# Moving VectorE's chord additions to GpSimd as 64-bit adds, and LN2's rstd to VectorE, in a fused attention and gated-MLP kernel

## The chip, the cores and the metric

The kernel runs on one core of one Trainium2 chip. The metric is device microseconds of one execution; lower is better. Each version is run several times and the median is quoted. A ratio is the mean time of one kernel's fast runs over that of the other's fast runs in the same rounds on the same chip, so it is not quite the ratio of the medians quoted beside it.

Names: PE is the matmul engine, ACT is ScalarE, DVE is VectorE, POOL is GpSimd. PSUM is the on-chip memory in which PE leaves its results here; SBUF is the one that holds the other tiles.

## The reference, cut to what matters

```python
h  = x + attention(layernorm(x), wqkv, wo)           # S = 2048, D = 512, 32 heads of 16
h2 = h + (sigmoid(g) * u) @ w_down                   # g, u = layernorm(h) @ w_gate, w_up;  F = 1792
```

Softmax runs over 32 heads of 2048 x 2048 scores. The exponentials of these scores are most of ACT's work. The first layernorm is called LN1 here, and the one on h is LN2. The rstd of a layernorm is one over the standard deviation of a row.

## The kernel before: the parts that matter

The scores of 128 keys by 512 queries make one *tile*. A *round* computes two or three tiles on PE. ACT exponentiates them in one instruction, or hands one tile of three to DVE. DVE builds its exponential from an integer trick. A first pass turns the score into the bits of an fp16 number. Two *chords*, the same bits plus a constant, are then added, and all three are multiplied by V with suitable weights, so their sum approximates the exponential. A DVE tile costs PE three multiplications where an ACT tile costs one.

```python
CHORDS, WEIGHT = (326, -332), 1.5625
...
def dexp_first(src, u, n):                  # first pass: PSUM scores -> int16
    ...
    nc.vector.tensor_scalar(out=J[:, 0, k, :], in0=src, scalar1=ZOFF, scalar2=0.0, op0=ALU.add, op1=ALU.max)
    T["D"] = max(T["D"], sc_end[n] + LAT) + 601
    ...
    uns = [Unit(u, J[:, s, k, :].bitcast(FP16), n, None if s else T["D"] + TAIL["D"],
                v=Vaug2 if s == 2 else Vaug) for s in range(3)]
    ...                                     # after up to four tiles: dexp_rest
def dexp_rest():
    ...
    def chord(s):                           # DVE adds the chord to k tiles at once
        nc.vector.tensor_scalar(out=J[:, s, 0:k, :], in0=J[:, 0, 0:k, :], scalar1=float(CHORDS[s - 1]),
                                scalar2=0.0, op0=ALU.add, op1=ALU.max)
        for i in range(k):
            quad[i][s].end = T["D"] + TAIL["D"]
    for s in (1, 2):
        chain.append((70 + 133 * k, lambda s=s: chord(s)))
```

The order of every engine's instructions is fixed when the program is built. A greedy scheduler in Python keeps a clock `T` per engine, adds an assumed cost for every instruction, and places next on PE whatever it believes to be ready. `Unit.end` is the time at which it believes an operand to be ready. On the chip, PE executes that order and waits wherever the belief was wrong. The assumed constants (601 ns, `70 + 133 * k`, `TAIL`) therefore decide the order.

```python
TAIL = {"A": 150.0, "D": 85.0, "G": 100.0}
def av_ready(loose):                        # which tiles may be multiplied by V now
    return [un for un in avq if un.u[:2] == gseq[st["cur"]] and un.end is not None
            and un.end + LAT <= T["P"] + loose]
```

The rstd of both layernorms is computed on GpSimd (an add, then a power of -0.5). GpSimd also makes the identity matrix at the start, on which everything depends.

## Time and profile before

781.5 us, median of 3.

| | busy us | share |
|---|---|---|
| PE | 730.5 | 94% |
| ACT | 735.3 | 94% |
| DVE | 708.5 | 91% |
| POOL | 29.8 | 4% |

The head of the profile's page: span, busy time of each engine, and the shares of the engines in the chain of waits that ended last.

```profile
span 779.7 us, 25718 instructions
...
PE 730.5 (94%) x11270; PEld 348.8 (45%) x11350; DVE 708.5 (91%) x1402; ACT 735.3 (94%) x780; POOL 29.8 (4%) x67
...
PE 48%; DVE 25%; ACT 21%; issue 5%; POOL 1%; DMA 0%; ACTq 0%; DVEq 0%
```

Three engines are nearly full, and the chain passes among them. PEld, the weight loads, has 11350 records and PE only 11270. 80 matmuls are missing from this trace, and their time reads as idle. The costliest groups on ACT and DVE (line, engine, operation, output and input, count, busy us, mean ns, idle before and its releasers):

```profile
L1346 ACT ACTIVATE pt<-PS 128x1024 f16<-128x1024 f32 (+1 forms) x516 | 544.5, 1161 | 10.9 <-PE PS L1031 4.3
L1202 DVE TENSOR_SCALAR J<-PS 128x512 int16<-128x512 f32 x545 | 360.2, 678 | 26.7 <-PE PS L1179 10.7
...
L1220 DVE TENSOR_SCALAR J<-J 128x2048 int16<-128x2048 int16 (+3 forms) x326 | 183.6, 594 | 0.8
```

L1220 is the work that the change moves: 326 chord additions, 183.6 us.

Busy time in stretches of 100 us (columns: stretch, its length, PE, PEld, DVE, ACT, POOL with instruction counts, PE clock, DMA share, GB/s):

```profile
300.00:400.00 100.00, 95.59 (x1640) 48.14 (x1646) 96.27 (x190) 98.24 (x105) 1.92 (x5) 1.00 0.21 62
600.00:700.00 100.00, 96.18 (x1676) 46.98 (x1680) 94.31 (x185) 97.79 (x103) 2.34 (x4) 0.98 0.18 54
```

The timelines of POOL and of ACT (start, duration, instruction):

```profile
0.73 0.20 POOL masks.py:197 MEMSET ident_bf<- 128x128 bf16 x1 [0.29 <-POOLq L1531]
1.01 0.29 POOL masks.py:199 TENSOR_SCALAR_AFFINE_SELECT ident_bf<-ident_bf 128x128 bf16<-128x128 bf16 x1
...
12.48 1.02 ACT L1346 ACTIVATE pt<-PS 128x1024 f16<-128x1024 f32 x1
```

The identity is ready at 1.3 us, and the first exponential starts at 12.48 us.

### The profile page before, as it was taken

The numbers are of one execution on the slowest core, as the hardware profiler recorded it, in microseconds if no ns is written. First come the engines' busy times: TensorE is split into PE (matmuls) and PEld (weight loads), VectorE is DVE, ScalarE is ACT, GpSimd is POOL, SyncE is SP. The second block draws the span as 40 slices with busy tenths as digits, with TensorE's granted clock in tenths as the row PEclk, the third lists the DMA queues.
The fourth block names the chain that finished last, engine by engine and source line by source line (L and its number), as shares of the span: only waits on it lengthen the run. The fifth ranks groups of instructions, "written<-read, shape, count | busy, mean of one in ns | idle before, by whom it ended". The sixth has DMA issues, their size and how long they took to land.

```text
span 779.7 us, 25718 instructions
## 1 busy us (share of the span) xinstructions
PE 730.5 (94%) x11270; PEld 348.8 (45%) x11350; DVE 708.5 (91%) x1402; ACT 735.3 (94%) x780; POOL 29.8 (4%) x67
## 2 busy tenths in 40 slices
PE   8899998988899999999999999999999999999997
PEld 3322223444454445544545455445543454345554
DVE  7987999999899899989999899998999999899863
ACT  5979999999999999999999999999999999999962
POOL 4300000000000000000000000100000000000000
PEclk9999999999999999999999999999999999999999
DMA  7000004000122103200211122101311123012160
GB/s 230 1 0 2 1 21 145 2 3 2 43 69 80 32 3 97 84 29 29 59 53 56 35 77 84 46 18 40 93 56 35 36 84 110 8 37 83 29 204 17
DMA packets 66806, 41.56 MB, mean 53 GB/s; under 512 B 3456, under 2 KB 66688, under 8 KB 66688
## 3 DMA queue, kind: packets, MB, share of 16 engines
q1 hardware_dynamic: 66400, 39.59, 17.1%
q8 instruction: 90, 1.47, 0.8%
q10 hardware_dynamic: 288, 0.26, 0.1%
q14 instruction: 28, 0.23, 0.1%
HBM read 37.75 MB, written 2.10 MB: 51 GB/s over the span
## 4 chain that ended last, share of the span: by engine, by line
PE 48%; DVE 25%; ACT 21%; issue 5%; POOL 1%; DMA 0%; ACTq 0%; DVEq 0%
ACT pt L1346 16%; PE PS L1031 16%; PE PS L1179 14%; DVE J L1202 11%; PE PS L770 8%; PE PS L788 5%; DVE J L1220 4%; PE PS L287 2%; DVE st L260 2%; DVE xs L1097 1%; ACT QTb L1346 1%; ACT xnT_83 L1346 1%; DVE hT L842 1%; ACT th L800 1%; DVE Vaug L296 1%
## 5 line engine op out<-in xcount | busy, mean ns | idle before, releaser
L1346 ACT ACTIVATE pt<-PS 128x1024 f16<-128x1024 f32 (+1 forms) x516 | 544.5, 1161 | 10.9 <-PE PS L1031 4.3
L1202 DVE TENSOR_SCALAR J<-PS 128x512 int16<-128x512 f32 x545 | 360.2, 678 | 26.7 <-PE PS L1179 10.7
L1179 PE MATMUL PS<-pt,Vaug 128*17 128x256 f16 (+1 forms) x2164 | 199.4, 279 | 3.6 <-DVE xs L1097 2.7
L1179 PE MATMUL PS<-J,Vaug 128*17 128x256 f16 (+1 forms) x2084 | 195.3, 279 | 4.3 <-DVE xs L1097 1.7
L1220 DVE TENSOR_SCALAR J<-J 128x2048 int16<-128x2048 int16 (+3 forms) x326 | 183.6, 594 | 0.8
L1179 PEld LDWEIGHTS <-Vaug 128*17 128x17 bf16 x4882 | 125.9, 90 | 74.0 <-issue 67.9
L1179 PE MATMUL PS<-J,Vaug_100 128*17 128x256 f16 (+1 forms) x1042 | 117.7, 279 | 0.7 <-DVE J L1220 0.6
L770 PE MATMUL PS<-xnT_82,wgu 128*128 128x256 bf16 x784 | 113.5, 275 | 0.6 <-DVE qd L699 0.2
L770 PEld LDWEIGHTS <-wgu 128*128 128x128 bf16 x784 | 63.9, 97 | 39.9 <-issue 34.3
L1179 PEld LDWEIGHTS <-Vaug_100 128*17 128x17 bf16 x1042 | 48.7, 90 | 27.4 <-issue 26.3
L1346 ACT ACTIVATE xnT_83<-PS 128x1024 f16<-128x1024 f32 (+1 forms) x51 | 57.0, 1119 | 0.2 <-PE PS L1031 0.2
L788 PE MATMUL PS<-wd,hT 128*128 128x512 bf16 x167 | 50.7, 383 | 3.4 <-issue 3.2
L1031 PEld LDWEIGHTS <-KT_86 32*128 32x128 bf16 x768 | 21.6, 91 | 61.4 <-issue 59.6
L1031 PEld LDWEIGHTS <-KT_87 32*128 32x128 bf16 x1024 | 25.5, 92 | 52.6 <-issue 50.7
L1031 PEld LDWEIGHTS <-KT_88 32*128 32x128 bf16 x1024 | 24.4, 92 | 50.3 <-issue 49.3
L1346 ACT ACTIVATE QTb<-PS 128x1024 f16<-128x1024 f32 x42 | 45.6, 1085 | 1.3 <-PE PS L1031 0.9
L800 ACT ACTIVATE th<-PS 128x512 f32<-128x512 f32 (+1 forms) x63 | 38.0, 603 | 7.5 <-DVE hT L783 6.7
L1031 PE MATMUL PS<-QT_92,KT_87 32*128 32x256 bf16 x512 | 38.6, 274 | 5.4 <-ACT pt L1346 3.5
L1031 PEld LDWEIGHTS <-KT_89 32*128 32x128 bf16 x1024 | 24.3, 92 | 42.0 <-issue 41.2
L1031 PE MATMUL PS<-QT_93,KT_87 32*128 32x256 bf16 x512 | 37.4, 272 | 2.8 <-ACT pt L1346 1.8
L1346 ACT ACTIVATE xnT_84<-PS 128x1024 f16<-128x1024 f32 (+1 forms) x36 | 38.8, 1091 | 0.9 <-PE PS L1031 0.8
L1031 PE MATMUL PS<-QT_95,KT_88 32*128 32x256 bf16 x512 | 37.2, 272 | 2.2 <-ACT pt L1346 1.7
(289 smaller groups left out, 808.4 us busy)
## 6 DMA issues: line engine op xcount, KB each, us to landing
wgu<-in_B_w_gate_dram SPq DMA_DIRECT2D x49, 256.0 KB, 3.0
wgu<-in_B_w_up_dram SPq DMA_DIRECT2D x49, 256.0 KB, 3.4
out_dram<-ob SPq DMA_DIRECT2D x16, 128.0 KB, 1.7
wd<-in_B_w_down_dram SPq DMA_DIRECT2D x1, 1792.0 KB, 9.3
xr<-in_A_x_dram SPq DMA_DIRECT2D x14, 128.0 KB, 3.6
J<-in_B_w_gate_dram SPq DMA_DIRECT2D x2, 768.0 KB, 4.5
J<-in_B_w_up_dram SPq DMA_DIRECT2D x2, 768.0 KB, 6.2
xb_111<-in_A_x_dram SPq DMA_DIRECT2D x2, 256.0 KB, 5.3
```

What stands on the lines that cost most here:

```text
L260: nc.vector.bn_stats(out=st[:], in_=src)
L287: nc.tensor.matmul(ps, lhsT=w_sb[:, d, p * P:(p + 1) * P], rhs=xnT[c][:, d, :], start=(d == 0), stop=(d == DC - 1))
L296: nc.vector.tensor_copy(out=Vaug[:, t, :, 0:DH], in_=ps.rearrange("p (h d) -> p h d", d=DH))
L770: nc.tensor.matmul(ps[:, 0:PARTS[r][2]], lhsT=w[:, d, :], rhs=hn_of(r)[:, d, :], start=(d == 0), stop=(d == DC - 1))
L788: nc.tensor.matmul(ps, lhsT=hT[:, f, i * P:(i + 1) * P], rhs=wd[:, f, :], start=(f == 0), stop=(f == FC - 1))
L800: nc.scalar.activation(out=th[:, 0:ps.shape[-1]], in_=ps, func=ACT.Tanh, scale=0.5)
L842: nc.vector.scalar_tensor_tensor(out=hT[:, f:f + k, 0:w], in0=th[f][:].rearrange("p (k n) -> p k n", k=k), scalar=1.0, in1=ps2.rearrange(" ...
L1031: nc.tensor.matmul(pss[:, ui, i * CW[qc]:(i + 1) * CW[qc]], lhsT=KT[g // 2][32 * j:32 * j + 32, k * P:(k + 1) * P], rhs=q[32 * j:32 * j + ...
L1179: nc.tensor.matmul(dst[32 * j:32 * j + VW, 0:w], lhsT=un.v[:, kt * SPAN[qc] + i, h, :], rhs=un.ap[:, i * w:(i + 1) * w], start=clears and ...
L1202: nc.vector.tensor_scalar(out=J[:, 0, k, :], in0=src, scalar1=ZOFF, scalar2=0.0, op0=ALU.add, op1=ALU.max)
L1220: nc.vector.tensor_scalar(out=J[:, s, 0:k, :], in0=J[:, 0, 0:k, :], scalar1=float(CHORDS[s - 1]), scalar2=0.0, op0=ALU.add, op1=ALU.max)
L1346: ex = nc.scalar.activation(out=pt, in_=pss[:, 0:wa, :], func=ACT.Exp, scale=AS)
```

## The change

The intent is to take the chords off DVE, which is 91% busy, and give them to GpSimd, which is 96% idle. The constant is added to four int16 values at once, as one 64-bit add. The first pass gets a floor of 332, so that no 16-bit field borrows from its neighbour. LN2's rstd leaves GpSimd and becomes six one-column DVE operations (a bit-trick guess and two Newton steps). After LN1, GpSimd does nothing but 64-bit adds.

```diff
+    def rstd_steps(dst, var):
+        ...                                  # guess(): v = var + eps; y = bits(v) * -0.5 + magic
+        def newton(i, s):
+            ...
+            nc.vector.tensor_scalar(out=t[:], in0=src, scalar1=src, scalar2=v[:], op0=ALU.mult, op1=ALU.mult)
+            nc.vector.tensor_scalar(out=out, in0=t[:], scalar1=3 * s * s, scalar2=src,
+                                    op0=ALU.subtract, op1=ALU.mult)
+        return guess, lambda: newton(0, scale), lambda: newton(1, -2 * scale ** 3)
...
-            jr.append(rstd_job(rstd[:, i:i + 1], mv[:, i, 1:2], j))
+            for part in rstd_steps(rstd[:, i:i + 1], mv[:, i, 1:2]):
+                j = dve(TINY, part, j)
+            jr.append(j)
...
-        nc.vector.tensor_scalar(out=J[:, 0, k, :], in0=src, scalar1=ZOFF, scalar2=0.0,
+        nc.vector.tensor_scalar(out=J[:, 0, k, :], in0=src, scalar1=ZOFF, scalar2=float(-min(CHORDS)),
...
+        def chord64(s):
+            nc.gpsimd.int64_add(words(s), words(0), CHORDS[s - 1] * (1 + 2 ** 16 + 2 ** 32 + 2 ** 48))
+            for i in range(k):
+                quad[i][s].end = T["G"] + TAIL["G"]
+        st["on_pool"] = st["on_pool"] or started() and not st["pows"]
         for s in (1, 2):
-            chain.append((70 + 133 * k, lambda s=s: chord(s)))
+            if st["on_pool"]:
+                gq.append(Job(150 + 192 * k, lambda s=s: chord64(s), [Mark(T["D"] + TAIL["D"])]))
+            else:
+                chain.append((70 + 133 * k, lambda s=s: chord(s)))
```

(Cut: the bookkeeping of `started()` and `pows`, the helper `words()`, two small changes of when the queues are emptied, and a dependency added to the scheduler's model of the output transposes.)

More of the change, by code (lines that the diff above doesn't have):

```diff
@@ L14 @@
 I32 = mybir.dt.int32
+I64 = mybir.dt.int64
 ALU = mybir.AluOpType
@@ L268, in rstd_of, with guess @@
         nc.gpsimd.tensor_tensor(out=dst, in0=v[:], in1=power[:], op=ALU.pow)
+    def rstd_steps(dst, var):
+        v = small.tile([P, 1], FP32, name="nv")
+        y = [small.tile([P, 1], FP32, name=f"ny{i}") for i in range(2)] + [dst]
+        t = small.tile([P, 1], FP32, name="nt")
+        scale = 2.0 ** (-4 / 9)
+        def guess():
+            nc.vector.tensor_scalar(out=v[:], in0=var, scalar1=1e-5, scalar2=None, op0=ALU.add)
+            nc.vector.tensor_scalar(out=y[0][:].bitcast(I32), in0=v[:].bitcast(I32), scalar1=-0.5,
+                                    scalar2=1597463007.0 - 4 / 9 * 2 ** 23, op0=ALU.mult, op1=ALU.add)
+        def newton(i, s):
+            src, out = y[i][:], (y[i + 1][:] if i == 0 else dst)
+            nc.vector.tensor_scalar(out=t[:], in0=src, scalar1=src, scalar2=v[:], op0=ALU.mult, op1=ALU.mult)
+            nc.vector.tensor_scalar(out=out, in0=t[:], scalar1=3 * s * s, scalar2=src,
+                                    op0=ALU.subtract, op1=ALU.mult)
+        return guess, lambda: newton(0, scale), lambda: newton(1, -2 * scale ** 3)
     def new_st():
@@ L523, in rstd_job, with power @@
     def rstd_job(dst, var, *deps):
-        gq.append(Job(800, lambda: rstd_of(dst, var), deps))
+        st["pows"] += 1
+        def power():
+            st["pows"] -= 1
+            rstd_of(dst, var)
+        gq.append(Job(800, power, deps))
         job = gq[-1]
@@ L527, in rstd_job @@
         return job
+    TINY = 330.0
     st = {"n": 0, "cur": 0, "pm": None, "mark": None, "acc": [None, None], "left": 0.0, "mode": None,
-          "R": 3, "ring": -1, "pms": [], "acts": deque(), "open": None, "item": None}
+          "R": 3, "ring": -1, "pms": [], "acts": deque(), "open": None, "item": None, "xs": None, "pows": 0, "on_pool": False}
     def dve(ns, fn, *deps, pr=0):
@@ L1097, in finish_group @@
         j = dve(650 - ns[0], lambda: nc.vector.transpose(
-            out=xs[:, 0:w // 32, :].rearrange("p b r -> p (b r)"), in_=src), Mark(T["P"] + DRAIN), pr=-1)
+            out=xs[:, 0:w // 32, :].rearrange("p b r -> p (b r)"), in_=src), Mark(T["P"] + DRAIN), st["xs"], pr=-1)
         for k in halves:
             st["acc"][k] = j
-        j = dve(690 - ns[1], norm, j)
+        j = st["xs"] = dve(690 - ns[1], norm, j)
         if a:
@@ L1223, in chord, with words @@
                 quad[i][s].end = T["D"] + TAIL["D"]
-        for s in (1, 2):
-            chain.append((70 + 133 * k, lambda s=s: chord(s)))
+        def words(s):
+            return J[:, s, 0:k, :].rearrange("p a b -> p (a b)").bitcast(I64)
+        def chord64(s):
[3 more added lines that the diff above has]
+        st["on_pool"] = st["on_pool"] or started() and not st["pows"]
+        for s in (1, 2):
+            if st["on_pool"]:
+                gq.append(Job(150 + 192 * k, lambda s=s: chord64(s), [Mark(T["D"] + TAIL["D"])]))
+            else:
+                chain.append((70 + 133 * k, lambda s=s: chord(s)))
+        run_pool()
     def pop_chain():
@@ L1230, in pop_chain, with started @@
         f()
+    def started():
+        return all(("ap", c) in done for c in range(1, NQC))
     def want_dve(n):
@@ L1288, in p_slots @@
                 dexp_rest()
-            pop_chain()
+            if chain:
+                pop_chain()
     lns = {c: early_ln(c) for c in range(1, NQC)}
```

## The prediction

> **What bounds it now.** Three engines share the limit. Table of windows, 140 to 740 us: ACT 98.5% busy, PE 95.1%, DVE 94.1%. ACT's figure flatters it: successive 1024-wide exponentials list 1.08 us each but can start 0.90 us apart (timeline), so part of the record is waiting. The chain of waits changes hands: overall PE 48%, DVE 25%, ACT 21%. From 600 to 620 us it is PE alone; from 300 to 330 us it is mostly DVE, with "J" first passes 39% and chord adds 15% of the chain. Startup (20 us) and tail (from 740 us) are untouched.
>
> **What the change removes, adds, moves.**
> - DVE loses all 326 chord adds: 183.6 us (groups table; 681 ns for 128x2048).
> - With DVE free the kernel's scheduler hands it more tiles. The instruction order of the two kernels shows first passes 545 -> 579 and score rounds unchanged at 694: 120 -> 85 three-tile and 569 -> 605 two-tile exponentials. DVE gains 34 x 0.66 = 22 us.
> - Six tiny DVE operations for each of 14 LN2 rows: 84 at about 0.17 us (bn_aggr takes 0.176): 14 us. DVE falls from 708 to about 560 us (72%).
> - ACT, at starts 0.90 and 1.33 us apart: -35 x 1.33 + 36 x 0.90 = about -14 us.
> - PE: each DVE tile is multiplied three times, an ACT tile once: 68 more units, about 3.7 us at a quarter of 0.216 us each; 16 fewer warming matmuls return 3.5 us. Net zero.
> - GpSimd: 340 64-bit adds, mostly 512 words per partition. The Trainium skill ("GPSIMD Engine Reference", Performance versus the Vector engine) gives 769 ns for 512 elements in a tight loop. Estimate from it: 0.95 us each with overhead, about 290 us in all, 37% of the span. No run here has shown this instruction yet. The 14 LN2 pow pairs leave GpSimd.
>
> **Port sharing.** The skill ("GPSIMD Engine Reference", Specifications) says GpSimd contends with two-port VectorE modes. The trace agrees: at 400.00 us a tiny GpSimd add took 0.57 us beside a 128x2048 chord add that ended at 400.49; alone it takes 0.22. The change removes most such VectorE work itself; what remains is small (Q splits, two-input norms). I expect little slowing of either engine.
>
> **Critical part.** The 184 us are not the gain. Where DVE leads the chain, ACT (0.90 to 1.0 us a round) and PE stand close behind. Chord adds are 3.7% of the chain (29 us), of which perhaps half returns; ACT's 14 us overlaps that. PE, hardly changed, then limits: it idles about 35 us between 60 and 740 us, and I expect 10 to 15 of these back. Gain 12 us.
>
> **Time: 769.5 us, 762 to 779 (8 in 10).** Chances: faster by over 2% 0.30, within 2% 0.65, slower 0.05.
>
> **What would show each step.** DVE busy near 560 us; no J<-J on DVE; GpSimd near 290 us, a 512-word add 0.9 to 1.1 us; ACT busy down 10 to 25 us; PE busy within 8 us of 730; the chain showing DVE under 15% and PE above 50%; PE idle in the middle down by 10 us or more; most gain before 600 us, where DVE led, and nearly none from 600 to 700 us. First passes stay near 0.68 us beside GpSimd.
>
> **What would make it wrong.** The adds being slower than planned, or a slow library load at the first: then PE, whose order is fixed, waits on J from GpSimd and the gain is lost. Port contention stretching the first passes. PE so near its own floor that freed DVE time yields only 3 to 5 us. On the good side: DVE's jitter causing more of PE's and ACT's stalls than its chain share shows; then 755 to 762 us.

## More of the kernel before

From one chip to the next the kernel before had medians of 779.7 to 781.7 us. Versions that ran in different calls are therefore compared by their ratios to the kernel before.

## The result and the profile after

788.8 us (median of 4, 788.75 to 790.63) against 781.5: ratio 1.010, 95% interval 1.0083 to 1.0118. The kernel became 1% slower. The prediction was a gain of 12 us, and the result lies above its range.

The head of the page of the changed kernel:

```profile
span 786.9 us, 26382 instructions
...
PE 745.8 (95%) x11460; PEld 351.4 (45%) x11460; DVE 606.0 (77%) x1194; ACT 724.2 (92%) x780; POOL 324.2 (41%) x379
...
PE 68%; DVE 15%; ACT 11%; issue 4%; POOL 2%; DVEq 0%; POOLq 0%; ACTq 0%
```

The work moved as announced. DVE lost 102 us of busy time, ACT lost 11 us, and DVE's share of the chain fell from 25% to 15%. Its groups:

```profile
L1394 ACT ACTIVATE pt<-PS 128x1024 f16<-128x1024 f32 (+1 forms) x519 | 536.0, 1123 | 19.5 <-PE PS L1062 14.7
L1260 POOL INT64_ADD J<-J x340 | 308.4, 920 | 398.3 <-DVE J L1233 357.5
L1233 DVE TENSOR_SCALAR J<-PS 128x512 int16<-128x512 f32 x579 | 384.8, 681 | 105.4 <-PE PS L1210 50.5
```

DVE now idles 105 us in front of its first passes, waiting for PE, where it used to idle 27 us. ACT's idle time before its main group rose from 10.9 to 19.5 us. The same two stretches:

```profile
300.00:400.00 100.00, 97.67 (x1643) 47.83 (x1638) 77.71 (x155) 96.62 (x103) 42.22 (x47) 1.00 0.20 58
600.00:700.00 100.00, 97.79 (x1631) 47.28 (x1626) 79.16 (x153) 97.77 (x105) 45.33 (x50) 1.00 0.20 59
```

DVE is far emptier, and ACT issues no more instructions per stretch than before. PE looks fuller, but that is mostly missing records: before_int64, a run below with the order of the kernel before and all its matmuls recorded, has PE busy for 97.3 and 97.5 us in the same stretches (counted 9.4 us later, as it starts later). The start explains the sign of the result:

```profile
0.73 0.20 POOL masks.py:197 MEMSET ident_bf<- 128x128 bf16 x1 [0.29 <-POOLq L1579]
9.14 0.28 POOL masks.py:199 TENSOR_SCALAR_AFFINE_SELECT ident_bf<-ident_bf 128x128 bf16<-128x128 bf16 x1 [8.21 <-issue]
...
21.19 1.02 ACT L1394 ACTIVATE pt<-PS 128x1024 f16<-128x1024 f32 x1
```

GpSimd sits 8.21 us between the memset and the identity, with nothing that the profile shows, and the first exponential starts 8.7 us later than before. I split the span by the exponentials of the two traces:

| | before | after | difference |
|---|---|---|---|
| start to first exponential | 12.5 | 21.2 | +8.7 |
| first exponential to end of last | 733.9 | 730.7 | -3.2 |
| end of last exponential to end | 33.3 | 35.0 | +1.7 |
| span | 779.7 | 786.9 | +7.2 |

Each column is one execution. The main phase of before_int64 is 730.9 us, so even the gain of 3.2 us is not clear of how one order varies between executions.

So there are two questions. Why did the start grow, and why did the main phase gain at most 3 us where 12 were expected?

A second sum describes the main phase. In both traces two exponentials in a row start no closer than about 0.90 us (two tiles) or 1.33 us (three tiles). Counting each ACT instruction at such a floor (0.48 and 0.26 us for the two sizes of tanh), ACT needed 699 us in the main phase before and 684 after, 15 us less, as predicted. The time between starts beyond the floors, ACT's gaps, rose from 34 to 45 us. Eleven of the fifteen microseconds turned into gaps.

### The profile page after: what moved, and what is told of

It is laid out like the page before. It is cut to its first block, busy times and chain, and to the rows that moved or that the text cites. A ratio compares the mean times of both kernels' runs of the same rounds, so it can differ in the third digit from the quotient of the medians.

```text
span 786.9 us, 26382 instructions
## 1 busy us (share of the span) xinstructions
PE 745.8 (95%) x11460; PEld 351.4 (45%) x11460; DVE 606.0 (77%) x1194; ACT 724.2 (92%) x780; POOL 324.2 (41%) x379
## 4 chain that ended last, share of the span: by engine, by line
PE 68%; DVE 15%; ACT 11%; issue 4%; POOL 2%; DVEq 0%; POOLq 0%; ACTq 0%
PE PS L1210 22%; PE PS L1062 21%; PE PS L801 12%; ACT pt L1394 8%; PE PS L819 6%; DVE J L1233 6%; PE PS L309 3%; POOL J L1260 2%; PE PS L740 2%; DVE xs L1128 1%; DVE st L261 1%; ACT xnT L1394 1%; PE PS L314 1%; PE PS L1541 1%; DVE Vaug L318 1%
## 5 line engine op out<-in xcount | busy, mean ns | idle before, releaser
L1394 ACT ACTIVATE pt<-PS 128x1024 f16<-128x1024 f32 (+1 forms) x519 | 536.0, 1123 | 19.5 <-PE PS L1062 14.7
L1260 POOL INT64_ADD J<-J x340 | 308.4, 920 | 398.3 <-DVE J L1233 357.5
L1062 PE MATMUL PS<-QT,KT 32*128 32x256 bf16 (+1 forms) x3712 | 266.4, 276 | 8.7 <-ACT pt L1394 3.7
L1210 PE MATMUL PS<-J,Vaug 128*17 128x256 f16 (+1 forms) x3315 | 240.3, 280 | 4.9 <-POOL J L1260 2.1
L1062 PEld LDWEIGHTS <-KT 32*128 32x128 bf16 x3840 | 91.8, 92 | 196.5 <-issue 192.6
L801 PE MATMUL PS<-xnT,wgu 128*128 128x256 bf16 x784 | 113.7, 275 | 1.7 <-DVE h L769 0.8
L1394 ACT ACTIVATE xnT<-PS 128x1024 f16<-128x1024 f32 (+1 forms) x87 | 96.5, 1138 | 1.7 <-PE PS L1062 1.5
L1210 PE MATMUL PS<-xnT,Vaug 128*17 128x256 f16 x368 | 54.6, 274 | 0.0
L873 DVE SCALAR_TENSOR_TENSOR hT<-th,PS 128x512 bf16<-128x512 f32 x49 | 33.3, 680 | 12.9 <-PE PS L801 11.8
L1128 DVE STREAM_TRANSPOSE xs<-PS 128x256 f32<-128x256 f32 (+1 forms) x60 | 27.6, 461 | 13.6 <-PE PS L1210 13.1
L1210 PE MATMUL PS<-QTb,Vaug 128*17 128x256 f16 (+1 forms) x162 | 28.0, 278 | 0.7 <-DVE xs L1128 0.7
```

The source lines that it names most:

```text
L801: nc.tensor.matmul(ps[:, 0:PARTS[r][2]], lhsT=w[:, d, :], rhs=hn_of(r)[:, d, :], start=(d == 0), stop=(d == DC - 1))
L873: nc.vector.scalar_tensor_tensor(out=hT[:, f:f + k, 0:w], in0=th[f][:].rearrange("p (k n) -> p k n", k=k), scalar=1.0, in1=ps2.rearrange(" ...
L1062: nc.tensor.matmul(pss[:, ui, i * CW[qc]:(i + 1) * CW[qc]], lhsT=KT[g // 2][32 * j:32 * j + 32, k * P:(k + 1) * P], rhs=q[32 * j:32 * j + ...
L1128: j = dve(650 - ns[0], lambda: nc.vector.transpose(out=xs[:, 0:w // 32, :].rearrange("p b r -> p (b r)"), in_=src), Mark(T["P"] + DRAIN), ...
L1210: nc.tensor.matmul(dst[32 * j:32 * j + VW, 0:w], lhsT=un.v[:, kt * SPAN[qc] + i, h, :], rhs=un.ap[:, i * w:(i + 1) * w], start=clears and ...
L1260: nc.gpsimd.int64_add(words(s), words(0), CHORDS[s - 1] * (1 + 2 ** 16 + 2 ** 32 + 2 ** 48))
```

## The experiments

**Theories.** *Library theory* for the start: the compiled program has an instruction that reloads GpSimd's library 0 ahead of the identity, and the changed one has another that loads library 1 ahead of its first 64-bit add (both are called `PseudoReloadLibraryIndex` in the built program). If the library stays as an execution leaves it, each execution of the changed kernel begins with the wrong one. For the main phase there were at first two theories: *PE floor* (PE had no slack, so freeing DVE gains little) and *GpSimd cost* (waits for chords and contention gave the gain back). A third, *order scatter*, came out of the second set of runs.

All times are medians; ratios are to the kernel before on the same chip.

### The start: two runs

`restore_late` is the changed kernel with one tiny GpSimd operation after the last 64-bit add. `before_int64` is the kernel before with one 64-bit add at its end.

```diff
# restore_late
+    nc.gpsimd.tensor_scalar(out=last_lib[:], in0=eps_t[:], scalar1=1.0, scalar2=None, op0=ALU.mult)
# before_int64
+    nc.gpsimd.memset(word[:], 0)
+    nc.gpsimd.int64_add(word[:].bitcast(I64), word[:].bitcast(I64), 1)
     bad = small.tile([P, 1], FP32, name="bad")
```

> The changed kernel plus one tiny GpSimd tensor_scalar after the last 64-bit add, so that the program ends with the standard GpSimd library resident. Library theory (an execution that ends with the 64-bit-add library resident makes the next one reload the standard library ahead of the identity mask, seen as an 8.2 us gap before it): the gap vanishes, the first exponential starts near 12.5 us instead of 21.2, time 780 us (779 to 781.5). Rival (the 8.2 us gap is something else, such as the size of the program or the input DMAs of the start slowing GpSimd): gap stays, time near 789 us.

> The kernel before plus one 64-bit add on 8 bytes at its very end on GpSimd; nothing else differs. Library theory: the next execution must reload the standard library, so a gap of about 8.2 us appears before the identity mask, the first exponential moves from 12.5 to about 21 us, time near 790 us, with not one exponential's work moved. Rival: no change, 781 to 782 us.

Measured: restore_late 779.95 us, ratio 0.9997 (0.9976 to 1.0017), first exponential at 13.2 us; before_int64 790.20 us, ratio 1.0139 (1.0112 to 1.0167), first exponential at 21.9 us. Both are as the library theory expected. The timeline of POOL in restore_late:

```profile
1.23 0.29 POOL masks.py:199 TENSOR_SCALAR_AFFINE_SELECT ident_bf<-ident_bf 128x128 bf16<-128x128 bf16 x1 [0.29 <-POOL ident_bf masks.py:197]
...
741.26 2.15 POOL L1260 INT64_ADD J<-J  x2 [2.93 <-DVE rsum L1098]
754.21 0.26 POOL L1548 TENSOR_SCALAR lastlib<-eps_t 128x1 f32<-128x1 f32 x1 [10.80 <-issue]
```

and in before_int64:

```profile
9.20 0.28 POOL masks.py:199 TENSOR_SCALAR_AFFINE_SELECT ident_bf<-ident_bf 128x128 bf16<-128x128 bf16 x1 [8.26 <-issue]
```

The library theory holds. The kernel before has the reload of library 0 too, and there it leaves a gap of 0.08 us, since that library is still in place. Eight bytes added at the end of an execution put an 8.26 us gap at the start of the next. A restore at the end of the changed kernel takes its gap away; the 10.80 us that the reload then takes are hidden behind the tail of the kernel. (The 1.39% of before_int64 is about 2 us more than its gap; that rest is not explained.) The remaining riddle is that the repaired kernel only ties with the kernel before.

### The main phase with nothing put in DVE's place

`free_before` and `free_after` keep each kernel's order but leave out the chord additions, and all three matmuls of a DVE tile read the first pass's result. The numbers are wrong. Their size is close enough that the comparison with the reference still passed, which says nothing about the kernel.

```diff
-        uns = [Unit(u, J[:, s, k, :].bitcast(FP16), n, None if s else T["D"] + TAIL["D"],
+        uns = [Unit(u, J[:, 0, k, :].bitcast(FP16), n, None if s else T["D"] + TAIL["D"],
...                                         # and the tensor_scalar / int64_add of the chord is left out
```

> The kernel before, same order on every engine, but the 326 chord adds are left out and the three matmuls of a DVE tile all read the first chord (wrong result on purpose, of similar size). It gives what removing 184 us of DVE work is worth with nothing put in its place. PE-floor theory (PE had little slack, so the freed DVE only uncovers PE): main phase shrinks by 3 to 12 us, time 770 to 778. Rival (DVE's chord work was what held the kernel, and GpSimd's longer latency gave it back): 15 us or more, time under 766.

> The changed kernel, same order on PE, ACT and DVE, but the 340 GpSimd adds are left out and the three matmuls read the first chord (wrong result on purpose); no library is switched. PE-floor theory: main phase (first exponential to end of last) near that of the changed kernel, 726 to 731 us against 730.7, and time 775 to 780. Rival (waits on GpSimd's chords and contention with GpSimd cost the main phase): main phase 720 us or less, time under 770.

Measured: free_before 776.46 us, ratio 0.9954 (0.9935 to 0.9972); free_after 771.08 us, ratio 0.9887 (0.9864 to 0.9911). Free_before is where the PE-floor theory put it; free_after fell between its two theories. Free_before's page:

```profile
span 774.8 us, 25459 instructions
...
PE 737.3 (95%) x11350; PEld 348.6 (45%) x11350; DVE 559.8 (72%) x1076; ACT 733.1 (95%) x780; POOL 27.5 (4%) x67
```

Taking all chords off DVE at an unchanged order is worth 0.46%, about 3 us, although DVE was a quarter of the chain. The order of the changed kernel with free chords is worth 1.13%, and the real GpSimd adds take 1.1% of the time back (0.9887 to 0.9997). Four steps make up the account (their sum is right by construction): -0.46% (chords off DVE), -0.67% (the other order, with 34 more DVE tiles and LN2 on DVE), +1.10% (the adds on GpSimd), +1.03% (the reload), together +1.00%. The second step mixes several parts of the change, which were not separated.

### What the adds cost: waits or contention

`pool_unread` runs all the adds, restores the library at the end, and lets the matmuls read the first pass's result as above. Nobody on PE waits for GpSimd, but GpSimd is as busy as ever.

> The changed kernel with the standard library restored at the end, all 340 GpSimd adds still run, but the matmuls read the first chord instead of what GpSimd writes (wrong result on purpose). The order on every engine is that of restore_late (779.95 us) and of free_after (771.08, no adds at all). Waiting theory (PE waits for chords that GpSimd delivers later than the order assumes): time falls back to 770 to 774 us although DVE's busy time stays near 606. Contention theory (GpSimd slows DVE's two-input and bf16 operations, 14 us of DVE busy time): time stays at 778 to 781.

Measured: 777.47 us, ratio 0.9953 (0.9925 to 0.9980). It lies between: from free_after (0.9887) to here, 0.66% is the price of GpSimd running at all; from here to restore_late (0.9997), about 0.44% is PE waiting for chords, though those two intervals just touch. Part of the contention is visible on DVE. First the kernel before, then the changed kernel, then free_after (the changed order without adds), for the same two operations:

```profile
L1068 DVE TENSOR_TENSOR o_1_105<-xs,rsum 128x128 bf16<-128x128 f32 x32 | 9.4, 292 | 1.1
...
L300 DVE TENSOR_SCALAR QT_95<-qd,mask 128x512 bf16<-128x512 bf16 x4 | 1.4, 344 | 0.0
```

```profile
L1099 DVE TENSOR_TENSOR o<-xs,rsum 128x128 bf16<-128x128 f32 x56 | 23.1, 413 | 1.9
L322 DVE TENSOR_SCALAR QT<-qd,mask 128x512 bf16<-128x512 bf16 x28 | 14.3, 529 | 0.1
```

```profile
L1099 DVE TENSOR_TENSOR o<-xs,rsum 128x128 bf16<-128x128 f32 x56 | 16.4, 292 | 1.9
L322 DVE TENSOR_SCALAR QT<-qd,mask 128x512 bf16<-128x512 bf16 x28 | 9.2, 346 | 0.1
```

The two-input normalisation went from 292 to 413 ns, and the bf16 split from 344 to 529. These means mix two cases. In the changed kernel's trace, 19 of the 56 normalisations overlap no add and took 292 ns on average; the other 37 took 474, one of them 967. Of the 28 splits, the 8 beside no add took 340 ns and the other 20 took 605. The first passes, which read PSUM, stayed at 681 ns. The Trainium skill ("GPSIMD Engine Reference", Specifications) says that GpSimd shares SBUF interfaces with VectorE and contends with VectorE instructions that have two SBUF inputs or a two-port mode, and the first of these two lines agrees. In total DVE is 14 us busier than without adds (606.0 against 592.3). That all of the 0.66% comes this way is not shown.

### Is PE the floor?

`light_pe_after` is restore_late with every second matmul of the down projection left out in the main phase (wrong result).

```diff
-        for f in range(a, b):
+        for f in range(a, b, 2):
             nc.tensor.matmul(ps, lhsT=hT[:, f, i * P:(i + 1) * P], rhs=wd[:, f, :],
-                             start=(f == 0), stop=(f == FC - 1))
+                             start=(f == 0), stop=(f == FC - 2))
```

> restore_late with every second matmul of the down projection left out in the main phase (98 of 196, [...]21 us of PE; wrong result on purpose), the order otherwise kept. PE-floor theory: PE is what limits with DVE relieved, time falls by 10 to 21 us against restore_late, to 759 to 770. Rival (PE merely waits for others): it falls by less than 5 us.

Measured: 776.13 us, ratio 0.9937 (0.9908 to 0.9966). Taking about 21 us of work off PE (98 matmuls, which start 0.215 us apart in restore_late's trace) returned 0.60%, or 4.7 us. My PE-floor theory fails its own test: in this order PE is not the only limit either. A likely reading is that the rounds end now at PE, now at another engine (the chain of restore_late is 69% PE, 14% DVE, 11% ACT). As the run lightened one kind of matmul alone, it does not show what PE work elsewhere is worth.

### The LN2 part alone

`dve_chords` is the changed kernel with `st["on_pool"] = False`: chords stay on DVE, and LN2's rstd is on DVE too. The raised floor of the first pass and the added dependency of the transposes stay in it as well.

> The changed kernel with the chords kept on DVE throughout, so no 64-bit add and no library switch: it is the kernel before plus the LN2 part (rstd on DVE), the raised floor of the first pass and the extra dependency of the transposes. If the LN2 part alone costs, since DVE was 91% busy and gets 14 to 18 us more: 781 to 785 us. If harmless: 779 to 781.

Measured: 794.62 us, ratio 1.0183 (1.0151 to 1.0214). It is worse than either expectation. The six operations for 14 rows take 17.6 us of DVE, and the scheduler, seeing DVE full, gives it 538 tiles instead of 545. As its order is another one too, how much of the 14 us is LN2's work and how much is the order, or the floor and the dependency, stays open. LN2's rstd on DVE is no gift by itself; what it does is to keep GpSimd on one library after LN1.

### The order itself

`calibrated` corrects one constant of restore_late. The traced adds last 398, 611, 824 and 1038 ns (medians of the changed kernel for k = 1 to 4 tiles, found by matching the adds of the trace to those of the program in order); `185 + 213 * k` fits all four, and the scheduler assumes `150 + 192 * k`. One add with k = 4 in the changed kernel:

```profile
404.31 1.04 POOL L1260 INT64_ADD J<-J  x1 [2.02 <-DVE J L1233]
```

```diff
-                gq.append(Job(150 + 192 * k, lambda s=s: chord64(s), [Mark(T["D"] + TAIL["D"])]))
+                gq.append(Job(185 + 213 * k, lambda s=s: chord64(s), [Mark(T["D"] + TAIL["D"])]))
```

> restore_late with the cost that the kernel's own placement assumes for a GpSimd add corrected from 150 + 192 k ns to the traced 185 + 213 k (398, 611, 824, 1038 ns for k = 1 to 4); the order changes with it. Waiting theory: PE's matmuls are placed where chords are really ready, time 773 to 778. Contention theory: no gain, 779 to 782.

Measured: 767.77 us, ratio 0.984 (0.9814 to 0.9865), 12 us better than restore_late and outside both expectations. That was more than removing every wait for chords had brought (pool_unread, 0.44%), so it could not be only better timing. The next runs ask whether it is the better constant or just another order. `calib_low` moves the constant the wrong way, to `115 + 171 * k`. `calib_margin` is calibrated with `TAIL["G"]` at 400 instead of 100. `free_calibrated` is calibrated's order without adds, made as free_after was. `before_jitter` is the kernel before with `75 + 136 * k` in place of `70 + 133 * k` for its DVE chords.

> restore_late (779.95 us) with the assumed cost of a GpSimd add moved the wrong way, from 150 + 192 k to 115 + 171 k ns (799 for k = 4, where the trace shows 1038). The order changes too: 589 DVE tiles against 579 in restore_late and 590 in calibrated. Cost theory (the 12 us of calibrated, 767.8, come from placing matmuls where chords are really ready): more waits on GpSimd than in restore_late, 780 us or more. Order theory (any change of a constant reshuffles the greedy order, and more DVE tiles are what helps): 766 to 773 us, near calibrated.

> calibrated with chords counted as ready another 300 ns later; 587 DVE tiles. Cost theory: no chord is waited for, 765 to 771 us. Order theory: within 765 to 775 as well, by tile count. If it falls back to 778 or more, late placement itself costs (J buffers held longer).

> The order of calibrated on PE, ACT and DVE, but no GpSimd adds, and matmuls that read the first chord (wrong result on purpose). Against free_after (771.08 us) it gives what the order alone is worth, against calibrated (767.77) what the real adds cost in it. Cost theory: adds cost 1 to 4 us here instead of 8.9, so 764 to 767. Order theory: the adds still cost about 8 us, and the order itself is 10 us better, so 758 to 761.

> The kernel before with the cost that its placement assumes for a DVE chord add nudged from 70 + 133 k to 75 + 136 k ns (607 for k = 4 becomes 619); same work to within one tile (544 against 545), another order. It measures how much the order alone scatters. If the scatter is small: 778 to 783. If the order is worth many us by chance: outside that, which would make part of any difference between two such kernels luck.

Measured: calib_low 769.44 us (0.9857), calib_margin 760.71 (0.9750, 0.9720 to 0.9779), free_calibrated 761.27 (0.9756), before_jitter 785.07 (1.0070, 1.0035 to 1.0106). A constant moved the wrong way is as good as the right one, so the cost theory fails. (calib_margin is below both of its ranges.) A constant of the kernel before, nudged by 3 to 4%, costs it 5 us (for k = 4 it goes from 602 to 619 ns; the expectation's 607 is a slip). The adds still cost 0.84% in calibrated's order (0.9756 to 0.984), so the order itself is what improved.

Four more runs, and then two, measured how wide the scatter is. `after_nudge` and `after_nudge2` are restore_late with `155 + 192 * k` and `145 + 192 * k`; `nominal_margin` is restore_late with `TAIL["G"]` at 400; `before_nudge` has `65 + 133 * k`; `before_margin` counts DVE chords as ready 300 ns later; `free_margin` is calib_margin's order without adds.

> restore_late (779.95 us) with the assumed cost of a GpSimd add 155 + 192 k instead of 150 + 192 k ns: 5 ns, the same 579 DVE tiles. Scatter theory: the order of the changed kernel is an unlucky draw, this one lands at 764 to 776. Systematic theory: 5 ns change nothing, 778 to 782.

> restore_late with its cost formula unchanged, but GpSimd results counted as ready 300 ns later. Margin theory (a matmul placed later does not find its chord missing): 758 to 766, like calib_margin at 760.7. Scatter theory: anywhere from 760 to 780.

> The kernel before with its assumed cost of a DVE chord 65 + 133 k instead of 70 + 133 k ns, 547 DVE tiles against 545. Scatter theory: 774 to 790, not the same as 780. No scatter: 778 to 782.

> The kernel before with DVE chords counted as ready 300 ns later, chords otherwise as they were, 545 DVE tiles. If a margin helps whoever computes the chord: 770 to 776, and the 760.7 of calib_margin owes 5 us or more to it. If the margin is GpSimd's affair: 778 to 787.

> The order of calib_margin (760.71 us) on PE, ACT and DVE without the GpSimd adds; matmuls read the first chord (wrong result on purpose). If the margin removes the waits for chords: the adds cost at most 3 us here, so 757 to 761. If it only gave a luckier order: they cost 6 to 9 us as in the other two orders, so 752 to 755.

> restore_late with the assumed cost of a GpSimd add 145 + 192 k instead of 150 + 192 k ns, no margin, 583 DVE tiles against 579. Scatter theory: anywhere from 766 to 780. If the tile count is what tells: between calib_low (589 tiles, 769.4) and restore_late (579, 779.95), so 773 to 778.

| orders of the same kernel | us | ratio | DVE tiles |
|---|---|---|---|
| before, as given | 779.7 to 781.7 | 1 | 545 |
| before_jitter | 785.07 | 1.0070 | 544 |
| before_nudge | 783.69 | 1.0040 | 547 |
| before_margin | 782.80 | 1.0042 | 545 |
| changed, library repaired (restore_late) | 779.95 | 0.9997 | 579 |
| after_nudge | 778.64 | 0.9978 | 579 |
| after_nudge2 | 770.29 | 0.9868 | 583 |
| calib_low | 769.44 | 0.9857 | 589 |
| calibrated | 767.77 | 0.9840 | 590 |
| nominal_margin | 765.80 | 0.9819 | 587 |
| calib_margin | 760.71 | 0.9750 | 587 |

A step of 5 ns in one direction did next to nothing (after_nudge, as the theory without scatter had it), and the same step in the other direction brought 1.3% (after_nudge2). The order as given is the fastest of the four tried for the kernel before, and the slowest of the seven for the repaired changed kernel, though level with after_nudge within the noise. The five changed orders without a margin have a mean ratio of 0.991; the three of before without one have 1.004. Between the families lies about 1.3%, or 10 us, close to the predicted 12. The given pair hides it because it compares the best order found of one family with the worst of the other. That is a handful of orders, not a distribution.

More DVE tiles go with shorter times (579: 780; 583: 770; 587 to 590: 761 to 769), but the tile count is not a setting that I could vary alone, so it is not shown as the cause. The margin on GpSimd's results was followed by a gain in both pairs (780 to 766, 768 to 761) and not with DVE chords. Free_margin speaks against the obvious reason: 754.83 us (0.9672), so the adds still cost 0.78% with the margin. The margin did not remove their cost; it led to a better order. Whether it would do so again is open.

The head of calib_margin, the fastest correct version, which beats both kernels by over 2%:

```profile
span 759.0 us, 26413 instructions
...
PE 719.5 (95%) x11420; PEld 346.8 (46%) x11493; DVE 607.7 (80%) x1202; ACT 716.9 (94%) x780; POOL 328.8 (43%) x384
```

It has DVE and POOL as busy as in the changed kernel and 7 us less of ACT. By the same sum as above, ACT's gaps in the main phase are 30 us against 45.

## Why the prediction was wrong

- **"Startup (20 us) and tail (from 740 us) are untouched"** is the step that failed first. Startup grew by 8.7 us, which alone exceeds the whole loss of 7.3 us. I had listed "a slow library load at the first" add as a risk, and there it did cost nothing visible: in restore_late, which loads library 1 before its first add, the fiftieth exponential after the first comes at 52.9 us against 52.8 in free_after, which loads none. What I missed is that a library stays resident after the execution, so that the bill comes at the start of the next. The Trainium skill ("GPSIMD Engine Reference", Instruction dispatch) gives 5.95 us for such a load, with no visible profile instruction. The trace agrees on the invisibility; the gaps here were 8.2 and 10.8 us.
- **"Gain 12 us"** did not come in the given order even with the library repaired (0.9997). At an unchanged order the chords are worth 3 us, not half of 29 us. Chain share was the wrong measure of it. The prediction had this case among its risks ("freed DVE time yields only 3 to 5 us") and did not let it count.
- **"PE idles about 35 us ... I expect 10 to 15 of these back."** Most of what was to come back was never there. The same stretch of the kernel before, of before_int64 (the same order, no record missing) and of the changed kernel, in that order, with the columns of the stretches above (PE is the first after the length):

```profile
60.00:740.00 680.00, 644.63 (x10637) 308.84 (x10700) 637.80 (x1239) 669.89 (x695) 14.03 (x28) 1.00 0.17 48
60.00:740.00 680.00, 656.91 (x10639) 307.74 (x10640) 638.34 (x1240) 670.05 (x694) 14.29 (x30) 1.00 0.17 48
60.00:740.00 680.00, 659.00 (x10736) 308.93 (x10734) 540.23 (x1043) 659.63 (x694) 297.90 (x329) 1.00 0.17 48
```

  PE reads as idle for 35.4, 23.1 and 21.0 us. So 12 us of the 35 are the size of the missing records, and PE's idle time hardly changed. PE's busy time over the whole span tells the same: 730.5 us with 11270 matmuls, but 743.3 with all 11350 in before_int64, against 745.8 in the changed kernel. In restore_late and pool_unread, with the same order and 3 us apart in span or less, it reads 744.6 and 729.6, while the trace holds 11460 and 11386 matmuls of the same list. The Trainium skill ("Perfetto Trace Analysis", Identifying the Most-Contended Engine) calls matmul busy time a bad measure of how near a kernel is to the roofline, because matmuls are pipelined; what misled me here was another fault of it, the missing records.
- **ACT's 14 us less work** was right (15 by the floors), but 11 us turned into gaps. The sum had no term for gaps.
- **The cost of the adds.** "0.95 us each ... about 290 us in all": 1.04 us for 512 words and 308 us in all, right within 10%. What I left out is what they do to others: 1.1% of the time in the given order, 0.8% in two better ones.
- **"I expect little slowing of either engine."** DVE's two-input and bf16 operations slowed by 40 to 55% on average, and only where they ran beside an add. The first passes did stay near 0.68 us as predicted. On DVE's total (560 predicted, 606 measured) 14 us are contention and 3 to 4 us the tiny operations (17.6 instead of 14). Most of the rest is how busy time is counted: each first pass lists 0.68 us but in a full queue starts 0.60 us after the one before, so operations that used to overlap now count in full. Leaving all chords out lowered DVE's busy time by 149 us (708.5 to 559.8), not by their 184.
- **What no step contained.** The order of this greedy scheduler scatters: by 0.7% in the four orders of the kernel before, by 1.6% in the five changed ones without a margin. A prediction from costs can aim at the family of orders, and the size came out near there (about 10 us between the means of 3 and 5 orders, without the reload). That the predicted path led to it is not shown, and part of the agreement may be luck: the chords alone were worth 3 us, and PE's idle time did not come back. For one given order the error of such a prediction can hardly be smaller than the scatter. Even so, the orders alone would not have made the kernel slower; the reload did.

## What to carry to other kernels

When a change brings a new kind of GpSimd instruction, ask which library the program leaves behind, because the next execution pays for it at its start; end on the library that the start needs, where a reload is hidden. When a program's order comes from a scheduler with assumed costs, time several nudged orders of both versions before judging a change of a per cent or two. An engine at 91% and a quarter of the chain may be worth only half a per cent when two others are as full; test it by leaving the work out at an unchanged order. Before idle time of PE goes into a sum, compare the counts of matmuls and weight loads; a missing record looks like idle time.

## What the Trainium skill lacked or had wrong

- "GPSIMD Engine Reference", Instruction dispatch: it does not say that the resident library carries over from one execution to the next. Here one 8-byte add at the end of an execution put an 8.26 us gap at the start of the next. It gives 5.95 us for a load; the gaps here were 8.2 us at the start and 10.8 us at the end.
- "GPSIMD Engine Reference", Engine selection, tells of an exact add of 32-bit integers only; no page has the cost of the 64-bit add with a constant. Here it took 185 + 213 ns per 128 words of each partition (1038 ns for 512). The 769 ns that Performance versus the Vector engine gives for a tight loop over 512 elements was too low for it.
- "GPSIMD Engine Reference", Specifications, names the contention without a size. With GpSimd 41% busy, a two-input DVE operation took 413 ns on average where it took 292 in the same order without adds, and a bf16 one 529 instead of 346; beside an add the means were 474 and 605.
- "Perfetto Trace Analysis" has no word of missing records. Here 80 of 11350 matmuls were missing from one trace, and PE read as idle for 35.4 us where a complete trace of the same order has 23.1.
